# Stores of prepared weights, moved from the load queue (SyncE) to ScalarE's queue, behind the next unit's sign

## The chip, the cores and the metric

The kernel runs on one core of one Trainium2 chip. The metric is the device time of one execution in microseconds (us), given as the median of three runs. Beside it stands one profiled execution, with the times of every instruction on the engines: PE (TensorE, with PEld for its weight loads), DVE (VectorE), ACT (ScalarE), POOL (GpSimd) and SP (SyncE, whose instructions issue DMAs). A queue name with a q (SPq, ACTq) is an engine's sequencer, which issues DMAs.

## The reference

A soft-capped attention, a gated MLP on its output, and a second MLP with a cosine. All weights of the MLPs arrive as float64 pairs of words and are turned into float32 on the chip.

```python
scores = cap * np.tanh(scale * np.matmul(q, k.transpose(0, 1, 3, 2)) / cap)
attn = softmax(scores)                      # written out in the source, with + 1e-09
x = np.matmul(attn, v)                      # (4, 12, 448, 64) -> 1792 tokens x 768
gate = 1.0 / (1.0 + np.exp(-(x @ w_gate)))  # 768 x 1536
y = gate * (x @ w_val) @ w_out              # 1536 x 768
h = y @ w_in                                # 768 x 2048
out = (h * np.cos(h)) @ w_out2              # 2048 x 768
```

## The kernel before

The tokens are done in two halves of 896 (hf 0 and 1). The order of work, written out by hand, is: attention of half 0, first MLP of half 0 with attention of half 1 beside it, **first MLP of half 1 with the "background" beside it**, second MLP of half 1, second MLP of half 0. Matmuls run in pairs of high and low parts: every weight tile w has a high part (w[:, 0]) and a low part (w[:, 1]), and for each slice of 128 rows mm3 issues four matmuls with the high part and then two with the low part.

The weights are cut into 70 units of up to 128 x 768. Units 0 to 35 belong to the first MLP, units 36 to 69 (w_in as wi, w_out2 as wz) to the second. In the first pass a unit is loaded raw (768 KB, two words for each weight), converted, and the result is stored to a DRAM tile kept[u] (384 KB), from which the later half reads it back (`w_load`, tiles f) instead of converting it again. For units 36 to 69 this conversion is the work of `background()`: it runs one step at a time between the matmuls of the first MLP of half 1, in the seven places BESIDE_G of each gate and value tile and the nine places BESIDE_Y of each output tile, and what is left runs when that MLP is over. A unit takes four steps:

1. Abs of the raw words on ACT (L158) into a float tile fb.
2. Sign of the raw words in place on ACT (L160), and then the raw load of the next unit (L149, on SP).
3. Two conversions on DVE (L165, L167).
4. Two more on DVE (L171, L175).

The store of the unit before (L205) stands in step 1, behind the Abs of the next unit, on SP's queue. Its DMA waits for L175 of the unit that it stores.

At the same time the main line reads the stored units back: `w_load` (L142) brings f from kept; `w_split` makes the high part on ACT (L238) and the low part on POOL (L239), which give the weight tile w that PE uses. In the first MLP of half 1, w60 to w71 are the twelve half tiles of its output matmul (py, 36 matmuls each), and w72, w73, w74 belong to the first three hidden tiles (ph) of the second MLP. Each half of py ends with a `w_step`, which splits one more w and loads one more f.

Tiles f and fb share one pool of four buffers (FB = 4), so a new f or fb waits for the last reader of the buffer that it gets: a POOL subtraction (L239) where an f was in it, the landing of a store (L205) where an fb was. Which buffer it gets is settled when the program is built; the count that an instruction's wait names tells it. Raw tiles and w share a pool of seven. Each engine and each queue works its instructions off in the order of the program: an instruction that waits holds up all behind it.

After the output matmul of each tile m of half 1, ACT casts y (L590) and DVE subtracts (L591); ph of the second MLP needs all six y. Each ph is copied by ACT (h, L707), scaled (u, L684), rounded on DVE (L685, L686), and goes through a sine on ACT (L691, its table loaded first) before the next cast of a w.

Of the kernel before, what the change touches and what calls it, by code (L numbers as in the profile page):

```python
# [27 lines left out]
def softcap_attention_gated_mlp_cos_mlp(  # L28
# [18 lines left out]
    nc = tc.nc  # L47
# [77 lines left out]
    kept = [dram.tile([P, UW], F32, tag=f"kept{i}", name=f"kept{i}") for i in range(NU)]  # L125
# [6 lines left out]
    def f_tile(i):  # L132
        return fpool.tile([P, UW], F32, tag="f", name=f"f{i}")
# [12 lines left out]
    def raw_tile(u):  # L146
        name, src, nk, n = u
        t = wts.tile([P, UW, 2], I32, tag="w", name=f"{name}_raw")[:, : nk * n]
        nc.sync.dma_start(out=t.rearrange("p (k f) t -> p k f t", k=nk), in_=src)  # L149
        return t  # L150
# [5 lines left out]
    def signs(raw, g):  # L156
        hi = raw[..., 1].bitcast(F32)
        nc.scalar.activation(out=g, in_=hi, func=AF.Abs)  # L158
        yield
        nc.scalar.activation(out=hi, in_=hi, func=AF.Sign, bias=tiny)  # L160

    def convert(raw, g):
        lo, hi = raw[..., 0], raw[..., 1]
        gi = g.bitcast(I32)
        nc.vector.tensor_scalar(out=g, in0=g, scalar1=F64_MIN_HI, scalar2=F64_MAX_HI, op0=ALU.max, op1=ALU.min)  # L165
        yield
        nc.vector.tensor_scalar(  # L167
            out=gi, in0=gi, scalar1=4, scalar2=REBIAS, op0=ALU.logical_shift_left, op1=ALU.bitwise_xor
        )
        yield  # L170
        nc.vector.scalar_tensor_tensor(  # L171
            out=gi, in0=lo, scalar=28, in1=gi, op0=ALU.logical_shift_right, op1=ALU.bitwise_or
        )
        yield
        nc.vector.scalar_tensor_tensor(  # L175
            out=gi, in0=gi, scalar=1, in1=hi, op0=ALU.logical_shift_right, op1=ALU.bitwise_xor
        )
# [20 lines left out]
    def background():  # L198

        raw = {N1: raw_tile(unit[N1])}  # L200
        done = None

        def store():
            u, g = done
            nc.sync.dma_start(out=kept[u][:, : g.shape[1]], in_=g)  # L205
            there.add(u)

        yield
        for u in range(N1, NU):
            _, _, nk, n = unit[u]  # L210
            g = f_tile(f"b{u}")[:, : nk * n]
            c = signs(raw[u], g)
            next(c)
            if done:
                store()
            yield
            for _ in c:
                pass
            if u + 1 < NU:
                raw[u + 1] = raw_tile(unit[u + 1])  # L220
            yield
            c = convert(raw.pop(u), g)
            next(c)
            next(c)
            yield
            for _ in c:
                pass
            done = (u, g)
            yield
        store()  # L230

    def w_split():
# [493 lines left out]
    with tc.manual_schedule():  # L726
        nc.vector.memset(zeros, 0.0)
        nc.vector.reciprocal(out=tanh_scale, in_=cap_sb)
        nc.vector.tensor_scalar_mul(out=tanh_scale, in0=tanh_scale, scalar1=1.0 / float(D) ** 0.5)
        nc.scalar.activation(out=guard, in_=cap_sb, func=AF.Exp, scale=-1.0)  # L730
        nc.vector.tensor_scalar_mul(out=guard, in0=guard, scalar1=1e-9 / CP)
        att = [attention(hf) for hf in range(B // BH)]
        steps = 3 + (BH * NP + 1) * NC - LAST
        for _ in range(steps):
            next(att[0])
        mlp1(0, att[0], att[1])
        for _ in range(steps - len(BESIDE)):
            next(att[1])
        others = background()
        lead[0] = 2  # L740
        y = mlp1(1, att[1], others)
        y_first = []
        for _ in others:
            pass
        lead[0] = 3
        mlp2(1, y, y_again(y_first))
        mlp2(0, y_first, iter(()))
# [35 lines left out]
```

## Time and profile before

| | us |
|---|---|
| median of 3 runs (1223.87 to 1224.69) | 1224.36 |
| the profiled execution's own time | 1220.99 |
| its span, first to last instruction | 1219.2 |
| PE busy in the span | 1195.7 (98%) |
| DVE, ACT, POOL busy | 687.5, 592.3, 445.6 |

The profiled execution is 3.4 us under the median of the runs, and 1.8 us of it lie outside the span. TensorE's granted clock is 0.998 of full speed over the span. A busy share is a mean over stages; what a change in one stage is worth is read from the waits of that stage.

### The profile page before, as it was taken

The page shows a single profiled execution, that of the slowest core. Times are in us where ns is not written, and L with a number is a line of the kernel's source. Part 1 is how long each engine was busy: PE and PEld are TensorE (multiplying, and loading weights), DVE is VectorE, ACT ScalarE, POOL GpSimd, SP SyncE. Part 2 cuts the span into 40 slices and gives each one's busy share as a digit, 9 for nine tenths or more (in the row PEclk, how much of TensorE's full clock was granted, in tenths as well). Part 3 has the DMA queues.
Part 4 walks back from the last instruction along what each step waited for, and adds up shares of the span by engine and source line. Part 5 has one row for each costly group of instructions (what it writes and reads, how often), then busy time and mean ns, then how long its engine had stood idle before and what let it go on. Part 6 is the DMA issues. An engine that isn't in the chain of part 4 may idle for free.

```text
span 1219.2 us, 15898 instructions
## 1 busy us (share of the span) xinstructions
PE 1195.7 (98%) x6347; PEld 1033.7 (85%) x6347; DVE 687.5 (56%) x729; ACT 592.3 (49%) x664; POOL 445.6 (37%) x234
## 2 busy tenths in 40 slices
PE   8989999999999999999999998999999999999998
PEld 4444889999987555999999997899999999999998
DVE  6998688778732997556566574511514534024242
ACT  6886455444425885444444345533506345344250
POOL 2767123223314665223233222522514333335140
PEclk9999999999999999999999999999999999999999
DMA  6431565555833340275655674121211631213003
GB/s 157 124 99 49 163 219 166 168 168 169 231 131 104 86 135 4 90 225 177 220 169 188 212 231 160 55 65 43 64 59 33 200 104 46 72 33 100 18 27 98
DMA packets 127083, 148.17 MB, mean 122 GB/s; under 512 B 50081, under 2 KB 100641, under 8 KB 127009
## 3 DMA queue, kind: packets, MB, share of 16 engines
q1 hardware_dynamic: 126720, 147.09, 39.1%
q8 instruction: 50, 0.82, 0.3%
q14 instruction: 25, 0.20, 0.0%
q10 hardware_dynamic: 288, 0.07, 0.0%
HBM read 112.13 MB, written 35.00 MB: 121 GB/s over the span
## 4 chain that ended last, share of the span: by engine, by line
PE 75%; DVE 13%; ACT 4%; DMA 4%; issue 2%; SPq 1%; POOL 0%; DVEq 0%; ACTq 0%; POOLq 0%
PE po L638 17%; PE ph L517 16%; PE pg L517 13%; PE pv L517 12%; PE py L517 7%; PE pv L422 4%; PE s L393 3%; DVE r L441 2%; DMA wz_raw<-in_moe_w_out_dram 2%; PE more L638 1%; PE t L372 1%; DVE f L171 1%; PE den L438 1%; DMA wi_raw<-in_moe_w_in_dram 1%; DVE fb L171 1%
## 5 line engine op out<-in xcount | busy, mean ns | idle before, releaser
L239 POOL TENSOR_TENSOR w<-f,w 128x768 fp32r<-128x768 f32 (+1 forms) x140 | 269.5, 1931 | 662.4 <-ACT w L238 572.8
L638 PE MATMUL po<-w,z 128*128 128x384 f32 x1248 | 221.0, 335 | 1.9 <-POOL w L239 1.9
L638 PEld LDWEIGHTS po<-w,z 128*128 128x128 f32 x1248 | 216.8, 188 | 2.9 <-POOL w L239 2.8
L517 PE MATMUL pv<-x,w 128*128 128x448 f32 x864 | 180.0, 366 | 0.9 <-DVE sg L566 0.9
L517 PE MATMUL pg<-x,w 128*128 128x448 f32 x864 | 179.9, 366 | 0.0
L517 PE MATMUL py<-g,w 128*128 128x448 f32 x864 | 177.5, 366 | 0.0
L517 PEld LDWEIGHTS pv<-x,w 128*128 128x128 f32 x864 | 162.0, 188 | 15.9 <-issue 3.0
L517 PEld LDWEIGHTS pg<-x,w 128*128 128x128 f32 x864 | 162.0, 188 | 14.7 <-ACT p L396 0.7
L517 PEld LDWEIGHTS py<-g,w 128*128 128x128 f32 x864 | 161.7, 188 | 13.5 <-issue 1.0
L685 DVE TENSOR_SCALAR n<-u 128x896 f32<-128x896 f32 (+1 forms) x38 | 29.4, 773 | 181.6 <-ACT u L684 181.6
L238 ACT CAST w<-f 128x768 fp32r<-128x768 f32 (+1 forms) x140 | 112.2, 809 | 39.3 <-DVE f L175 16.2
L517 PE MATMUL ph<-y,w 128*128 128x448 f32 (+1 forms) x578 | 119.9, 369 | 3.3 <-ACT y L590 2.8
L517 PEld LDWEIGHTS ph<-y,w 128*128 128x128 f32 x578 | 109.3, 190 | 13.3 <-ACT y L590 3.2
L517 PE MATMUL ph<-ya,w 128*128 128x448 f32 (+2 forms) x579 | 118.2, 365 | 0.0
L517 PEld LDWEIGHTS ph<-ya,w 128*128 128x128 f32 x579 | 108.4, 188 | 9.1
L396 ACT ACTIVATE p<-s,tanh_scale 112x896 f32<-112x896 f32 x96 | 93.0, 1011 | 43.0 <-PE s L393 42.9
L402 ACT ACTIVATE p<-p,cap_sb 112x1792 f32<-112x1792 f32 x48 | 86.3, 1798 | 0.1
L393 PEld LDWEIGHTS s<-st 64*112 64x112 f32 x576 | 45.7, 171 | 40.9 <-ACT p L396 19.0
L422 PE MATMUL pv<-p,v 112*64 112x448 f32 x384 | 77.5, 545 | 2.7 <-PE t L372 2.7
L441 DVE RECIPROCAL r<-den 128x448 f32<-128x448 f32 x24 | 70.8, 2950 | 8.7 <-PE den L438 8.7
L393 PE MATMUL s<-st 64*112 64x448 f32 x576 | 73.3, 380 | 1.5 <-ACT p L396 1.4
L406 POOL TENSOR_TENSOR sum<-p 112x896 f32<-112x896 f32 x24 | 55.9, 2330 | 49.1 <-ACT p L402 24.1
(82 smaller groups left out, 1201.8 us busy)
## 6 DMA issues: line engine op xcount, KB each, us to landing
f<-kept SPq DMA_DIRECT2D x96, 384.0 KB, 3.1
kept<-f SPq DMA_DIRECT2D x36, 384.0 KB, 2.7
wi_raw<-in_moe_w_in_dram SPq DMA_DIRECT2D x16, 768.0 KB, 5.8
kept<-fb SPq DMA_DIRECT2D x30, 384.0 KB, 2.7
wz_raw<-in_moe_w_out_dram SPq DMA_DIRECT2D x14, 768.0 KB, 5.2
wg_raw<-in_moe_w_gate_dram SPq DMA_DIRECT2D x12, 768.0 KB, 4.9
wv_raw<-in_moe_w_val_dram SPq DMA_DIRECT2D x12, 768.0 KB, 5.2
wo_raw<-in_moe_w_out_dram SPq DMA_DIRECT2D x12, 768.0 KB, 4.8
```

The lines of the kernel that those rows point to most:

```text
L171: nc.vector.scalar_tensor_tensor(out=gi, in0=lo, scalar=28, in1=gi, op0=ALU.logical_shift_right, op1=ALU.bitwise_or)
L238: nc.scalar.copy(out=t[:, 0], in_=r)
L239: nc.gpsimd.tensor_tensor(out=t[:, 1], in0=r, in1=t[:, 0].bitcast(F32), op=ALU.subtract)
L393: nc.tensor.matmul(ps[:CP, h, :S], lhsT=st[r, ki, ks], rhs=st[r, qi], start=(n == 0), stop=(n == 2))
L396: nc.scalar.activation(out=pt[:CP, j], in_=ps[:CP, :, :S], func=AF.Tanh, scale=tanh_scale[:CP])
L402: nc.scalar.activation(out=pt[:CP], in_=pt[:CP], func=AF.Exp, scale=cap_sb[:CP])
L406: nc.gpsimd.tensor_tensor(out=s, in0=pt[:CP, 1] if half == 0 else s, in1=pt[:CP, 0], op=ALU.add)
L422: nc.tensor.matmul(pv[h * D : (h + 1) * D, :S], lhsT=tv[:, h, c, :], rhs=pt[:CP, j, h, :], start=(c == 0), stop=(c == NC - 1),)
L441: nc.vector.reciprocal(out=r[:, 0], in_=den[:, :S])
L517: nc.tensor.matmul(ps[:, c, s0:s1], lhsT=w[:, wi, kk, :], rhs=x[:, xi, c, s0:s1], start=(first and (wi, xi) == (0, 0)), stop=(last and (wi ...
L638: nc.tensor.matmul(pos_t[t][:, :NB], lhsT=zf[kk][:, zi, t * P : (t + 1) * P], rhs=ws[kk // UK][:, wi, kk % UK, :], start=(kk == 0 and (zi, ...
L685: nc.vector.tensor_scalar_add(out=n[:, c], in0=u[:, c], scalar1=ROUND)
```

## The change

The store's DMA is issued by ScalarE (`nc.scalar`) and no longer by SyncE, and it moves in the program from behind the Abs of the next unit to behind its Sign, one step later. Nothing is added or taken away: the same 34 stores move the same bytes.

```diff
         def store():
             u, g = done
-            nc.sync.dma_start(out=kept[u][:, : g.shape[1]], in_=g)
+            nc.scalar.dma_start(out=kept[u][:, : g.shape[1]], in_=g)
             there.add(u)
...
             c = signs(raw[u], g)
             next(c)
+            yield
+            for _ in c:
+                pass
             if done:
                 store()
-            yield
-            for _ in c:
-                pass
             if u + 1 < NU:
                 raw[u + 1] = raw_tile(unit[u + 1])
             yield
```

What the built programs show at three places. Names: f and w carry their place in the sequence, fb and kept the number of the unit, wz_1_1_2_raw is a raw tile; behind "waits" stand the semaphores, DMAHW for the landing of a DMA, Pool, DVE, PE and Activation for an engine's progress.

**Place 1: ACT, at the end of the first gated tiles of half 1 (unit 55 follows w61).** Before:

```order
L238 CAST w61_5276<-f61_5172 128x768 [waits DMAHW4_49]
L158 ACTIVATE fb55_5288<-wz_1_0_4_raw_5248 128x384 [waits DMAHW2_49,DMAHW0_49]
L160 ACTIVATE wz_1_0_4_raw_5248<-wz_1_0_4_raw_5248,tiny_165 128x384 [waits Activation_49]
L238 CAST w62_5328<-f62_5223 128x768 [waits DMAHW6_49]
L158 ACTIVATE fb56_5339<-wz_1_1_0_raw_5304 128x768 [waits DMAHW3_49,Pool_49]
```

Now:

```order
L238 CAST w61_5276<-f61_5171 128x768 [waits DMAHW4_49]
L158 ACTIVATE fb55_5288<-wz_1_0_4_raw_5248 128x384 [waits DMAHW7_49,DMAHW6_49,Pool_49]
L160 ACTIVATE wz_1_0_4_raw_5248<-wz_1_0_4_raw_5248,tiny_165 128x384 [waits Activation_49]
L205 DMA kept54_135<-fb54_5232 128x768 [waits DMAHW3_49]
L238 CAST w62_5328<-f62_5223 128x768 [waits DMAHW6_49]
L158 ACTIVATE fb56_5339<-wz_1_1_0_raw_5304 128x768 [waits DMAHW3_49,DMAHW2_49]
```

The store of unit 54 now stands between the Sign of unit 55 and the cast of w62. Since that store is issued later, the buffer of fb54 is not there for fb55: its Abs waited for the landing of kept54 and for its raw load, and waits now for POOL, by its count for the subtraction of w61.

**Place 2: SP, the loads around the raw load of unit 57 (wz_1_1_2).** Before:

```order
L142 DMA f64_5331<-kept28_109 128x768 [waits DMAHW4_49,Pool_49]
L205 DMA kept55_136<-fb55_5288 128x384 [waits DMAHW5_49,DVE_49]
L149 DMA wz_1_1_2_raw_5349<-in_moe2_w_out_dram 128x2x768 [waits DMAHW6_49]
L205 DMA kept56_137<-fb56_5339 128x768 [waits DMAHW7_49,DVE_49]
L142 DMA f65_5385<-kept29_110 128x768 [waits DMAHW1_49,DMAHW0_49,Pool_49]
```

Now:

```order
L149 DMA wz_1_1_0_raw_5304<-in_moe2_w_out_dram 128x2x768 [waits DMAHW2_49,Activation_49]
L142 DMA f64_5331<-kept28_109 128x768 [waits DMAHW6_49,DMAHW4_49,Pool_49]
L149 DMA wz_1_1_2_raw_5349<-in_moe2_w_out_dram 128x2x768 [waits DMAHW5_49,DVE_49]
L142 DMA f65_5384<-kept29_110 128x768 [waits DMAHW7_49,DMAHW1_49,Pool_49]
L149 DMA wz_1_1_4_raw_5398<-in_moe2_w_out_dram 128x768 [waits DVE_49]
```

The raw load stands directly behind the load of f64 and no longer behind the store of unit 55. By the counts of its waits f64 waited for the subtraction of w61 and waits now for that of w62, one tile later. For f65 and f66 the subtraction that they wait for is the same in both programs (w63, w64). In the same way f72 waits now for the subtraction of w70 (before: the landing of kept63) and f73 for that of w71 (before: the landing of kept65).

**Place 3: ACT, the end of the background, before the first hidden tile of the second MLP.** Before:

```order
L160 ACTIVATE wz_2_1_2_raw_5883<-wz_2_1_2_raw_5883,tiny_165 128x768 [waits Activation_49]
L238 CAST w73_5925<-f73_5819 128x768 [waits DMAHW2_49]
L590 CAST y1_5_5930<-py1_5_5824 128x896 [waits PE_49]
L158 ACTIVATE fb69_5937<-wz_2_1_4_raw_5923 128x384 [waits DMAHW1_49,DMAHW0_49,Pool_49]
L160 ACTIVATE wz_2_1_4_raw_5923<-wz_2_1_4_raw_5923,tiny_165 128x384 [waits Activation_49]
L707 COPY h1_0_5983<-ph1_0_5946 128x896 [waits PE_49]
```

Now:

```order
L160 ACTIVATE wz_2_1_2_raw_5883<-wz_2_1_2_raw_5883,tiny_165 128x768 [waits Activation_49]
L205 DMA kept67_148<-fb67_5862 128x768 [waits DVE_49]
L238 CAST w73_5925<-f73_5818 128x768 [waits DMAHW1_49]
L590 CAST y1_5_5930<-py1_5_5823 128x896 [waits PE_49]
L158 ACTIVATE fb69_5937<-wz_2_1_4_raw_5923 128x384 [waits DMAHW7_49,DMAHW0_49]
L160 ACTIVATE wz_2_1_4_raw_5923<-wz_2_1_4_raw_5923,tiny_165 128x384 [waits Activation_49,Pool_49]
L205 DMA kept68_149<-fb68_5913 128x768 [waits DVE_49]
L205 DMA kept69_150<-fb69_5937 128x384 [waits DVE_49]
L707 COPY h1_0_5983<-ph1_0_5946 128x896 [waits PE_49]
```

One store stands now ahead of the casts of w73 and y1_5, and two ahead of the copy of h1_0; the last of them waits for DVE's conversion of unit 69, which no instruction of ACT waited for before.

## Rows read from the trace of the kernel before

**Rows 1.** The page: part 1 (busy us), and the stores in part 6.

```profile
PE 1195.7 (98%) x6347; PEld 1033.7 (85%) x6347; DVE 687.5 (56%) x729; ACT 592.3 (49%) x664; POOL 445.6 (37%) x234
...
kept<-fb SPq DMA_DIRECT2D x30, 384.0 KB, 2.7
```

**Rows 2.** Timeline of PE: start, length, instructions merged, idle before and releaser.

```profile
651.27 87.71 PE L517 MATMUL py<-g,w 128*128 128x448 f32 x432
738.82 6.24 PE L517 MATMUL ph<-y,w 128*128 128x448 f32 x30
747.88 0.67 PE L517 MATMUL ph<-y,w 128*128 128x448 f32 x2 [2.82 <-ACT y L590]
...
758.78 29.90 PE L517 MATMUL ph<-y,w 128*128 128x448 f32 x144
```

**Rows 3.** Windows: busy us of PE, PEld, DVE, ACT, POOL; granted clock, DMA.

```profile
750.00:753.00 3.00, 3.00 (x10) 2.66 (x9) 2.86 (x6) 2.66 (x4) 0.00 (x0) 0.52 0.06 24
```

**Rows 4.** Waits of SP's queue: total us, times, longest.

```profile
SPq L205 <- DVE fb L175: 118.4, 30, 13.0
```

**Rows 5.** Timeline of SP's queue: start, length of the issue.

```profile
661.12 0.32 SPq L205 DMA_DIRECT2D kept<-fb  x1
661.49 0.43 SPq L149 DMA_DIRECT2D wz_raw<-in_moe_w_out_dram  x1
...
718.92 0.32 SPq L142 DMA_DIRECT2D f<-kept  x1
721.81 0.32 SPq L205 DMA_DIRECT2D kept<-fb  x1
722.22 0.38 SPq L149 DMA_DIRECT2D wz_raw<-in_moe_w_out_dram  x1
...
728.38 0.32 SPq L142 DMA_DIRECT2D f<-kept  x1
...
738.25 0.44 SPq L149 DMA_DIRECT2D wz_raw<-in_moe_w_out_dram  x1
```

**Rows 6.** Timeline of ACT at units 55 and 59 and behind the last y.

```profile
655.58 0.56 ACT L158 ACTIVATE fb<-wz_raw 128x384 f32<-128x384 f32 x1
...
685.57 0.82 ACT L238 CAST w<-f 128x768 fp32r<-128x768 f32 x1
...
746.93 0.90 ACT L590 CAST y<-py 128x896 fp32r<-128x896 f32 x1
...
750.54 0.91 ACT L707 COPY h<-ph 128x896 f32<-128x896 f32 x1 [0.33 <-PE ph L517]
751.34 1.01 ACT L684 ACTIVATE u<-ph,quarter 128x896 f32<-128x896 f32 x1
...
756.47 0.82 ACT L238 CAST w<-f 128x768 fp32r<-128x768 f32 x1
```

**Rows 7.** Timeline of POOL: subtractions of w61 and w62, w65, w70, w71, w74.

```profile
655.72 3.90 POOL L239 TENSOR_TENSOR w<-f,w 128x768 fp32r<-128x768 f32 x2 [7.93 <-ACT w L238]
...
686.47 1.85 POOL L239 TENSOR_TENSOR w<-f,w 128x768 fp32r<-128x768 f32 x1 [9.12 <-ACT w L238]
...
718.99 1.98 POOL L239 TENSOR_TENSOR w<-f,w 128x768 fp32r<-128x768 f32 x1 [4.42 <-ACT w L238]
727.35 1.86 POOL L239 TENSOR_TENSOR w<-f,w 128x768 fp32r<-128x768 f32 x1 [6.39 <-ACT w L238]
...
757.37 2.03 POOL L239 TENSOR_TENSOR w<-f,w 128x768 fp32r<-128x768 f32 x1 [8.45 <-ACT w L238]
```

**Rows 8.** Timeline of DVE: the end of the background and the first rounding.

```profile
753.36 0.56 DVE L175 SCALAR_TENSOR_TENSOR fb<-fb,wz_raw 128x384 int32<-128x384 int32 x1
753.83 0.62 DVE L685 TENSOR_SCALAR n<-u 128x896 f32<-128x896 f32 x1
```

**Rows 9.** Timeline of ACT's queue at the start: the only two DMAs that it issues.

```profile
0.74 0.39 ACTq L323 DMA_DIRECT2D ident<-in_eye_dram  x1
1.17 0.52 ACTq L327 DMA_DIRECT2D cap_sb<-in_cap_dram  x1
```

More of the change, by code (lines that the diff above doesn't have):

```diff
@@ L213, in background @@
             next(c)
-            if done:
-                store()
             yield
@@ L218, in background @@
                 pass
+            if done:
+                store()
             if u + 1 < NU:
```

## The prediction

> **What bounds the kernel now.** The page comes first: PE is busy 98% of the span [rows 1], so a change gains only where PE waits, and loses where it makes PE wait. The change touches the stretch from 497 us, the first background store, to 754 us, the last. In PE's timeline there is then one wait to be seen: the output matmul (py) runs through from 651.27 us, the first hidden tile (ph) begins at 738.82, and after 30 matmuls PE stands for 2.82 us until ACT has cast the last y [rows 2]. Behind that wait the granted clock is 0.52 in the window of 750 to 753, the lower of TensorE's two levels (1.2 of 2.4 GHz); ten matmuls run there instead of the 14.8 that 3 us hold at the pace below, some 1.0 us lost [rows 3]. More is not to be won here than these 3.8 us.
>
> What can be lost is read from margins. 432 matmuls of py start over 738.82 - 651.27 = 87.55 us, 0.2027 us each, so every half tile of 36 takes 7.30 us and w65, the sixth, is wanted at 651.27 + 5 x 7.30 = 687.75, its low part four matmuls later at 688.56 [rows 2]. The low part of w65 is ready at 686.47 + 1.85 = 688.32 [rows 7]: 0.24 us to spare. Likewise w74: wanted at 758.78, low part at 759.59 [rows 2], ready at 757.37 + 2.03 = 759.40 [rows 7]: 0.19 us. So the weights come just in time, and the question is whether ACT and POOL make them later.
>
> They follow a chain that goes round once for each half tile: a POOL subtraction ends and frees a buffer; SP loads an f into it and, 0.37 us behind, the next raw unit; the raw lands; ACT does Abs; only then, in its order, comes the next cast of a w, and POOL's next subtraction. The last turn shows it: a raw load is issued at 738.25 [rows 5], and the cast of the last y, which stands on ACT behind that unit's Abs, comes at 746.93 [rows 6], while PE waits.
>
> **The change part by part.**
>
> The issue. 34 stores leave SP's queue, 0.32 us each [rows 5], and with them SP's 118.4 us of waiting for DVE ahead of them [rows 4]. ACT gets 34 issues of 0.39 to 0.52 us, as its two at the start took [rows 9]; I take 0.4. 34 x 0.4 = 13.6 us in all, hidden in ACT's idle half, save where a store stands between Abs and a cast that PE waits for. The transfers themselves, 2.7 us to landing [rows 1], stay.
>
> What a store waits for on ACT. It waits for L175 of the unit before, which is mostly done when the Sign of the next is; nothing is added there, except at the end of the background (third step below).
>
> First step, the chain up to w65. The store is issued one step later, so its buffer comes free later, and the program gives f and fb other buffers. The Abs of unit 55 ran at 655.58 [rows 6]; it now waits for w61's subtraction, which ends at 655.72 + 1.95 = 657.67 (half of two, [rows 7]): 2.09 us later. With kept54's issue (0.4) behind it, w62's subtraction ends at 659.62 + 2.5 = 662.1, and f64 waits for that now. The raw load behind f64 goes at 662.1 + 0.05 + 0.37 = 662.5, where it went at 661.49, behind the store of 661.12 [rows 5]: 1.0 us late. For f65 and f66 nothing changes, so the delay goes through to w65, plus 0.4 for kept58's issue ahead of its cast: 1.4 us, the lower bound. Upstream of w61 the same exchange of buffers takes place; the largest one that I can read is f72's, 718.92 to the end of w70's subtraction at 720.97 [rows 5, 7], 2.05 us, so 3.5 us is the upper bound. I take the middle, 2.4. Then w65's high part is ready at 685.57 + 0.82 + 2.4 = 688.79 [rows 6], PE waits 1.0 us, and its low part at 690.72 while PE would want it at 689.60: 1.1 more. PE is 2.2 us late.
>
> Second step, the last y. f73 waits now for w71's subtraction, 727.35 + 1.86 = 729.21 [rows 7], where it went at 728.38 [rows 5]: 0.83 us, and the raw load, w72 and the next turn follow it. kept67's issue stands ahead of y's cast: 0.4. Nothing else late: 1.2 us, the lower bound. At f72 something is given back: its raw load went at 722.22, behind the store of 721.81 [rows 5]; now it goes at 720.97 + 0.4 = 721.4, 0.8 us sooner, plus whatever w70 is late. With 3.5 us late there: 3.5 - 0.8 + 0.83 + 0.4 = 3.9 us, the upper bound. I take the middle, 2.5 us. What PE lost at w65 doesn't add to this: PE comes to the place of the 2.82 us wait later by 2.2, y is later by 2.5, and it waits 3.1 there. The low clock behind it stays.
>
> Third step, w74. kept69 now waits on ACT for the conversion of unit 69, which ends at 753.36 + 0.56 = 753.92 [rows 8], and the copy of h1_0, which ran at 750.54 [rows 6], stands behind it: 753.92 + 0.05 + 0.4 = 754.37, 3.8 us later. u follows 0.80 later and takes 1.01 [rows 6], so the rounding starts at 756.18 and not at 753.83, when DVE came free of the background [rows 8]: 2.35 us later. From there to w74's cast it is as before, so its high part is ready at 756.47 + 0.82 + 2.35 = 759.64 [rows 6] and not by 758.78: PE waits 0.86. The low part is ready at 761.75, and wanted at 759.64 + 0.81 = 760.45: 1.3 more. Together 2.1 us, on top of the second step, because all these times move with y.
>
> The sum: 2.5 + 2.1 = 4.6 us. On the profiled execution, 1220.99, that is 1225.6; on the median of the runs, which lies 3.4 us above it, 1224.36 + 4.6 = 1229.0 us, 0.38% slower.
>
> On the transfers the Trainium skill (DMA: Bandwidth & Descriptors, section Issuing engines are not separate DMA queues) says that DMAs issued by ScalarE and SyncE end up on the same 16 DMA engines, and that a second issuer saves only the sequencer's time. No row before shows a store from ACT. By that sentence alone nothing would move in or out of PE's path, and the time would stay at 1224.4.
>
> **The rivals.**
>
> No change (0.26). Between the raw loads of units 57 and 68 there are twelve on the chain. If each lands 0.25 us sooner because no store sits right ahead of it on its queue, as at 721.81 and 722.22 [rows 5], the chain gets 3 us back: y is 0.5 us early, the third step still costs 2.1, and the time is 1226.0. For it: SP's waits for DVE are gone [rows 4]. Against it: f loads stand in the same place ahead of the raw loads, and on the rows read they now wait for a later subtraction.
>
> Faster (0.14), the same mechanism with more effect. By the first two sums total = delay of y + 2.1 us, since w74 hangs on the same chain. For a gain over 2.45 us, the 0.2% that a measurement here can tell from no change, y must be 4.6 us sooner than before, 7.1 us better than forecast, or 0.6 us for each of the twelve loads. Then 1221.8; the most is 1220.6, with all of the 3.8 us won. The skill (same page, section Queues, rings and completion order) says that SP and ACT each have a ring of their own on every DMA engine, served in turn packet by packet, by which a store would share with a raw load and not delay it as a whole; no run here shows it.
>
> Slower still (0.12). The first step at its upper bounds, y 3.9 us late, and a further stretch of low clock behind the new waits at w65 and w74, 1.0 us each as in [rows 3]: 3.9 + 2.1 + 2.0 = 8.0, 1232.4 us.
>
> **How the numbers follow.** The forecast itself, 2.5 to 7 us slower, has 0.48; with the rival beyond it slower has 0.60, the same 0.26, faster 0.14. The lower bounds of the terms (1.2 + 2.1) give 1227.7, the upper ones (3.9 + 2.1) 1230.4. The range for 8 in 10 takes in most of "no change" and the low clock: 1223.0 to 1233.5.
>
> **What the changed profile would show.** Step one right: PE waits of 1 us or more for the cast and the subtraction of w65 near 688 us; wrong: py without a gap. Step two right: the wait for the last y stays near 3 us and ends at 750 instead of 747.9; wrong: it is shorter, or the y cast comes before 746.9. Step three right: the copy of h1_0 stands behind the last two stores, and PE waits for w74; wrong: no wait for w there. The prediction fails as a whole if raw loads of the y stretch land in clearly less time than now, or if the store's issue on ACT takes far from 0.4 us.

## The result, and the profile after the change

The change makes the kernel slower. Five executions of the changed kernel have a median of 1233.78 us (1230.11 to 1236.21), five of the kernel before on the same chip 1224.69 us (1223.87 to 1226.86): 9.1 us by the medians. The ratio, estimated from all the executions and so not the quotient of the two medians (1.0074), is 1.0063 (95% interval 1.0048 to 1.0078), or 7.7 us. In all comparisons, executions that took over 1.5% longer than the fastest of the same kernel are left out. The forecast was 1229.0 us, 4.6 us slower, with a range up to 1233.5. The sign was right, and so were the places that it named. The size was 50 to 60% of what came; the median lies 0.3 us above the range, and the time by the ratio (1232.1) inside it. The profiled execution after took 1233.04 us (span 1231.2), 12.0 us more than the span before.

The page, parts 1 and 6: PE has 7.7 us more busy time, some of it matmuls at the low clock, and the stores are now issued by ACT's queue. They land a little sooner than before (2.3 us, where [rows 1] have 2.7).

```profile
PE 1203.4 (98%) x6347; PEld 1036.4 (84%) x6347; DVE 690.1 (56%) x729; ACT 592.3 (48%) x664; POOL 446.6 (36%) x234
...
kept<-fb ACTq DMA_DIRECT2D x30, 384.0 KB, 2.3
```

The timeline of PE after the change, the answer to [rows 2] (start, length, matmuls merged, idle before and releaser):

```profile
530.13 6.75 PE L517 MATMUL pv<-x,w 128*128 128x448 f32 x32 [0.46 <-POOL w L239]
545.21 6.75 PE L517 MATMUL pv<-x,w 128*128 128x448 f32 x32 [0.21 <-POOL w L239]
604.83 6.75 PE L517 MATMUL pv<-x,w 128*128 128x448 f32 x32 [0.86 <-POOL w L239]
...
655.19 37.04 PE L517 MATMUL py<-g,w 128*128 128x448 f32 x180
694.13 1.09 PE L517 MATMUL py<-g,w 128*128 128x448 f32 x4 [1.90 <-ACT w L238]
696.04 52.09 PE L517 MATMUL py<-g,w 128*128 128x448 f32 x248 [0.82 <-POOL w L239]
747.97 6.24 PE L517 MATMUL ph<-y,w 128*128 128x448 f32 x30
757.40 0.83 PE L517 MATMUL ph<-y,w 128*128 128x448 f32 x2 [3.19 <-ACT y L590]
...
769.21 1.08 PE L517 MATMUL ph<-y,w 128*128 128x448 f32 x4 [1.10 <-ACT w L238]
771.31 28.99 PE L517 MATMUL ph<-y,w 128*128 128x448 f32 x134 [1.02 <-POOL w L239]
```

Before, there was one wait in this stretch, beside the 0.45 us for DVE's part of the same y (0.30 now, in neither count). Now there are eight: three in the value tiles of the gated MLP, two at w65 (its high part 2.5 us late: 694.13 against 655.19 + 180 x 0.2027 = 691.68; its low part 1.1 more), the old one for the last y, and two at w74. Behind three of them TensorE runs at the lower of its two levels (1.2 of 2.4 GHz). Windows of the changed kernel, columns as in [rows 3]:

```profile
696.50:699.50 3.00, 3.00 (x10) 2.69 (x9) 2.92 (x4) 0.23 (x1) 0.00 (x0) 0.50 0.77 215
758.00:761.00 3.00, 2.70 (x8) 2.21 (x8) 2.90 (x5) 0.55 (x1) 0.45 (x1) 0.50 0.40 130
771.50:774.50 3.00, 3.00 (x9) 2.65 (x10) 1.45 (x2) 1.48 (x2) 3.00 (x2) 0.50 0.45 134
```

Where the 12.0 us of the profile arise is read from the same places in the two timelines:

| place | before | after | late by |
|---|---|---|---|
| gate tile ahead of the first background store | 490.76 | 491.49 | 0.73 |
| py starts | 651.27 | 655.19 | 3.92 |
| ph starts | 738.82 | 747.97 | 9.15 |
| PE gets the last y | 747.88 | 757.40 | 9.52 |
| PE gets w74's low part (before 758.78 + 4 x 0.2027) | 759.59 | 771.31 | 11.72 |

The first 0.73 us lie ahead of anything that the change touches, and some 0.7 us more are matmuls that ran at a slower pace until 529 us (below). So about 2.5 us are lost in the gated tiles, 5.2 in py, 0.4 at the last y and 2.2 at w74.

### The profile page after: what moved, and what is told of

Same layout as the page of the kernel before. It is cut to its first block, busy times and chain, and to the rows that moved or that the text cites. A ratio compares the mean times of both kernels' runs of the same rounds, so it can differ in the third digit from the quotient of the medians.

```text
span 1231.2 us, 15898 instructions
## 1 busy us (share of the span) xinstructions
PE 1203.4 (98%) x6347; PEld 1036.4 (84%) x6347; DVE 690.1 (56%) x729; ACT 592.3 (48%) x664; POOL 446.6 (36%) x234
## 4 chain that ended last, share of the span: by engine, by line
PE 66%; DVE 10%; DMA 8%; issue 6%; ACT 5%; POOL 3%; SPq 1%; ACTq 0%; POOLq 0%; DVEq 0%
PE po L638 17%; PE ph L517 16%; PE pv L517 8%; PE pg L517 8%; PE py L517 7%; DMA wz_raw<-in_moe_w_out_dram 4%; PE pv L422 4%; PE s L393 3%; POOL w L239 2%; DMA kept<-fb 2%; DMA wi_raw<-in_moe_w_in_dram 1%; DVE r L441 1%; PE more L638 1%; PE t L372 1%; ACT p L396 1%
```

## Where the chain falls behind first

The prediction began its first step at unit 55. The first slip stands 140 us earlier. Two loads on SP's queue, first in the kernel before and then in the changed one, with POOL's two subtractions of the changed kernel (w42 and w43):

```profile
515.91 0.32 SPq L142 DMA_DIRECT2D f<-kept  x1
...
522.81 0.32 SPq L142 DMA_DIRECT2D f<-kept  x1
```

```profile
518.31 0.34 SPq L142 DMA_DIRECT2D f<-kept  x1
...
530.11 0.32 SPq L142 DMA_DIRECT2D f<-kept  x1
```

```profile
515.73 2.55 POOL L239 TENSOR_TENSOR w<-f,w 128x768 fp32r<-128x768 f32 x1 [4.20 <-ACT w L238]
528.12 1.96 POOL L239 TENSOR_TENSOR w<-f,w 128x768 fp32r<-128x768 f32 x1 [9.84 <-ACT w L238]
```

The two f are f44 and f45. Before, by the counts of their waits, they got the buffers of fb37 and fb38 once those stores had landed, with the subtractions of w40 and w41 long done. When the program allots f44 now, the store of unit 37 has not been written yet, so f44 gets the buffer of f42 and waits for w42's subtraction: 515.73 + 2.55 = 518.28, and it goes at 518.31, 2.4 us late. The raw load stands behind it, the Abs behind the raw load, the cast of w43 behind the Abs: it comes at 527.15 and not at 523.52, and its subtraction ends at 530.08. PE is waiting for it (530.13 in the timeline above), and so is f45: 7.3 us late, and its raw load with it. Of these 7.3 us, 3.65 are the exchange at the old times (w43's subtraction ended at 526.46 before, and f45 went at 522.81); the other 3.6 are w43's own lateness. In that, 2.4 us come from the raw load that went later (518.70 and not 516.28), and 1.2 from its landing: its Abs starts 6.8 us behind the issue, 5.6 before. So transfers have a smaller part in it beside the buffers. By the wait counts the same exchange comes back eight units later at f52 and f53, at f60 and f61, at f64, and in the output matmul's stretch at f67, f69, f71, f72 and f75, each of which now waits for the subtraction of the w two before it (f73 too, see place 2).

## The experiments

Each ratio is against the kernel before on the same chip, five rounds. The spread of these is wider than in the first comparison; where an interval decides nothing, the waits of the trace are read.

| | place of the store | queue | other | ratio | 95% interval |
|---|---|---|---|---|---|
| change | behind Sign | ACT | | 1.0063 | 1.0048 to 1.0078 |
| 1 | old | ACT | | 1.0003 | 0.9980 to 1.0026 |
| 2 | behind Sign | SP | | 1.0097 | 1.0064 to 1.0130 |
| 3 | behind Sign | ACT | five f/fb buffers | 0.9941 | 0.9916 to 0.9966 |
| 4 | old | SP | five f/fb buffers | 0.9945 | 0.9919 to 0.9970 |
| 5 | behind Sign | ACT | last store on SP | 1.0018 | 0.9999 to 1.0037 |
| 5, again | | | | 1.0038 | 1.0021 to 1.0054 |
| 6 | old | ACT | last store on SP | 0.9979 | 0.9957 to 1.0001 |
| 7 | one step sooner than old | ACT | | 1.0016 | 0.9999 to 1.0032 |
| 8 | one step later than behind Sign | ACT | | 1.0045 | 1.0024 to 1.0066 |
| 9 | behind Sign up to unit 54, then old | ACT | | 1.0025 | 1.0006 to 1.0043 |
| 10 | old up to unit 54, then behind Sign | ACT | | 1.0022 | 1.0011 to 1.0032 |
| 11 | old | ACT | last two stores on SP | 0.9997 | 0.9979 to 1.0015 |

**1. The queue alone** (the only difference to the kernel before):

```diff
-            nc.sync.dma_start(out=kept[u][:, : g.shape[1]], in_=g)
+            nc.scalar.dma_start(out=kept[u][:, : g.shape[1]], in_=g)
```

> Half of the change: the store is issued on ScalarE, at its old place behind the Abs of the next unit. Theory P (place: the store comes a step later, its buffer comes free later, f and fb get other buffers, and the chain of raw loads is late by some microseconds): the chain is as before, only the last stores still stand ahead of the copy of h1_0, so 2.1 us: 1226.8, with the last y near 747 us and a PE wait for w74. Theory Q (queue: a store that waits for DVE on ACT holds up the casts behind it): a store that stands one step sooner waits for DVE longer, so at least as slow as the whole change, 1234 or more.

No change: 1.0003. The timeline of PE:

```profile
744.45 15.27 PE L517 MATMUL ph<-y,w 128*128 128x448 f32 x72
762.01 1.08 PE L517 MATMUL ph<-y,w 128*128 128x448 f32 x4 [2.29 <-ACT w L238]
764.11 30.47 PE L517 MATMUL ph<-y,w 128*128 128x448 f32 x140 [1.02 <-POOL w L239]
```

There is no wait for w in the gated tiles or in py, and none for the last y, which even [rows 2] have; the two waits at w74 are there. Two things weaken this reading. The execution ran at the slower of two paces that are told of at the end (py in 89.44 us, 87.71 in [rows 2]), so PE came later to the last y; run 6, the same program up to its last store, ran py in 87.71 us and waited 0.96 us for it. And the queue is not quite alone: in the built program 22 of the 174 f and fb tiles lie in another buffer than before (41 with the change), f47 to f49 and f55 to f57 among them. What is won here is won by the queue together with an allotment of its own. Theory Q falls: of stores that wait for DVE on ACT, the ratio and PE's waits show nothing but the third step. Theory P had the place right, but not that the chain would gain what the third step costs.

**2. The place alone** (the store on SyncE, but behind the Sign):

```diff
             c = signs(raw[u], g)
             next(c)
-            if done:
-                store()
             yield
             for _ in c:
                 pass
+            if done:
+                store()
```

> The other half: the store stays on SyncE, but stands behind the Sign, one step later. Theory P: the last y is late as in the whole change, the third step (the stores ahead of h1_0 on ACT) is gone: 1224.7 + 9.1 - 2.1 = about 1231. Theory Q: nothing waits on ACT for DVE, so 1224.7.

The slowest of all: 1.0097, some 12 us (its interval, 1.0064 to 1.0130, overlaps the change's). Theory Q falls; theory P has the direction right, and the size is above it. PE has six waits in the value tiles, of which the longest is shown, three in py (0.51, 1.72 and 0.82 us), and then the one for the last y:

```profile
610.40 6.75 PE L517 MATMUL pv<-x,w 128*128 128x448 f32 x32 [1.01 <-POOL w L239]
...
765.16 11.28 PE L517 MATMUL ph<-y,w 128*128 128x448 f32 x46 [4.12 <-ACT y L590]
```

So the late place costs, and by the ratios ACT's queue gives a part of it back. The exchange of buffers alone does not explain this run: in its program f44, f45, f52, f53, f60 and f61 change their buffers as with the change, but f64, f67, f69, f71, f72 and f75 have those of the kernel before. What is late there has to come from ahead, or from stores that land later. Also, store and raw load go out directly behind each other on one queue; the stores land in 4.0 us (2.7 before, 2.3 with the change) and the raw loads of the wz units in 6.0 (5.2 and 5.1). That this slower landing has a part in the 12 us is a rival that no run rules out.

**3 and 4. A fifth buffer for f and fb**, with the change and without it:

```diff
-    FB = 4
+    FB = 5
...
-    small = ctx.enter_context(tc.tile_pool(name="small", bufs=6))
+    small = ctx.enter_context(tc.tile_pool(name="small", bufs=4))
```

> The whole change with five f and fb buffers and not four (the small pool of the attention goes from 6 to 4 tiles to make room; the run of the kernel before with the same two pools is its control). Theory P: with a fifth buffer f and fb no longer wait for a store that comes late; only the third step is left, so 2.1 us over the control. Theory Q: the stores stand where they stood on ACT, so 9 us over the control.

> Control: the kernel before with five f and fb buffers and a small pool of 4. Both theories: the chain of the kernel before is just in time, so a fifth buffer wins back at most the 2.8 us wait for the last y and the 1.0 us of low clock behind it: 1221 to 1225; the smaller pool of the attention may cost something ahead of 465 us, which the start of the gated tiles of half 1 (471 us) shows.

Both are faster than the kernel before, 0.9941 and 0.9945, and the difference of 8 to 9 us between change and no change is gone, within intervals of 3 us either way. With the fifth buffer the late store keeps no one waiting: the timeline of PE with the change has py and 216 matmuls of ph without a gap, and ACT copies h1_0 when PE has made it, since the last conversion is done by then. A fifth buffer would hide a slower landing as well; that the buffers are the path is read at f44 and f45 above.

```profile
658.34 89.44 PE L517 MATMUL py<-g,w 128*128 128x448 f32 x432
747.62 44.80 PE L517 MATMUL ph<-y,w 128*128 128x448 f32 x216
```

```profile
752.93 2.25 ACTq L205 DMA_DIRECT2D kept<-fb  x2
755.26 0.91 ACT L707 COPY h<-ph 128x896 f32<-128x896 f32 x1 [5.39 <-PE ph L517]
```

Not even the third step is left, which theory P had wanted at 2.1 us. The timeline of run 4:

```profile
655.07 87.71 PE L517 MATMUL py<-g,w 128*128 128x448 f32 x432
742.62 43.94 PE L517 MATMUL ph<-y,w 128*128 128x448 f32 x216
786.39 1.40 PE L638 MATMUL po<-w,z 128*128 128x384 f32 x7
```

and the end of the same stretch in the kernel before, which begins at 738.82 [rows 2]:

```profile
788.52 1.38 PE L638 MATMUL po<-w,z 128*128 128x384 f32 x7
```

The 216 matmuls of ph take 43.77 us in run 4 and 49.70 before. So the wait for the last y, with what follows it (DVE's part of y, the low clock), cost the kernel before 5.9 us, and not the 3.8 that the prediction and the expectation of run 4 took for the most to be won. By its ratio run 4 gains some 6.7 us.

These are the only two versions clearly faster than the kernel before. The smaller pool of the attention was not run by itself; in run 4's profile py starts 3.8 us later than before.

**5. The change with the last store back on SyncE**, run twice; the trace read is that of the second time.

```diff
-        def store():
+        def store(q=nc.scalar):
             u, g = done
-            nc.scalar.dma_start(out=kept[u][:, : g.shape[1]], in_=g)
+            q.dma_start(out=kept[u][:, : g.shape[1]], in_=g)
...
-        store()
+        store(nc.sync)
```

> The whole change, but the last store alone (unit 69) goes back to SyncE, so that no instruction of ACT ahead of the copy of h1_0 waits for DVE's last conversion. Theory P (chain late by the buffers, plus the third step): the wait for the last y stays at about 3 us, the two waits for w74 (1.1 and 1.0 us in the changed kernel) and the low clock behind them (1.7 us) go: 3 to 4 us under the changed kernel, ratio to the kernel before 1.003. Rival R (w74 is late because its own f or its own subtraction is late, not because of the copy): the waits for w74 stay, and the time is that of the change, ratio 1.006.

> The change with the last store alone back on SyncE, once more, for an undisturbed trace (the first one held a run of 6110 us). Theory P: the copy of h1_0 comes some 3 us sooner after the last y than in the changed kernel, w74 is waited for by under 1 us or not at all, the wait for the last y stays near 3 us; ratio 1.002 to 1.003, as measured the first time. Rival R: waits for w74 as in the changed kernel (1.1 and 1.0 us).

1.0018 and 1.0038, under the change's 1.0063 both times, though the second interval (1.0021 to 1.0054) reaches into the change's. ACT in the changed kernel, from the Sign of unit 68 on:

```profile
754.86 0.97 ACT L160 ACTIVATE wz_raw<-wz_raw,tiny 128x768 f32<-128x768 f32 x1
754.87 0.33 ACTq L205 DMA_DIRECT2D kept<-fb  x1
755.74 0.81 ACT L238 CAST w<-f 128x768 fp32r<-128x768 f32 x1
756.46 0.90 ACT L590 CAST y<-py 128x896 fp32r<-128x896 f32 x1
...
761.56 2.25 ACTq L205 DMA_DIRECT2D kept<-fb  x2
763.85 0.91 ACT L707 COPY h<-ph 128x896 f32<-128x896 f32 x1 [5.30 <-DVE fb L175]
...
768.34 0.82 ACT L238 CAST w<-f 128x768 fp32r<-128x768 f32 x1
```

and in run 5, second time:

```profile
754.50 0.90 ACT L590 CAST y<-py 128x896 fp32r<-128x896 f32 x1
...
759.97 0.91 ACT L707 COPY h<-ph 128x896 f32<-128x896 f32 x1 [3.35 <-DVE fb L165]
...
764.47 0.82 ACT L238 CAST w<-f 128x768 fp32r<-128x768 f32 x1
```

From the last y to the cast of w74 it is 11.88 us with the change, 9.97 with the last store moved back, and 9.54 before [rows 6]. PE's waits at w74 are gone, those at w65 (2.2 and 0.8 us) and for the last y (3.2 us) are not. Rival R falls, and the third step is shown by itself.

**6 and 11. The queue alone, with the last store, or the last two, back on SyncE**: the same edit of `store` and of its last call as in 5, on run 1; for 11 the call in the loop is also `store(nc.sync if u == NU - 1 else nc.scalar)`.

> Queue alone (store on ScalarE at its old place), but the last store goes back to SyncE. With the queue alone the last y was not waited for, and w74 was, for 2.29 and 1.02 us. Theory P: both waits are gone, 3.3 us and the low clock behind them, some 4 to 5 us under the queue alone: ratio 0.996 to 0.997, faster than both kernels. Rival R: w74 is late by its own chain, the waits stay, ratio 1.000.

> Stores on ScalarE at the old place, the last two (units 68 and 69) on SyncE. With one alone moved back, the last y was waited for by 0.96 us and w74 still by 0.91 and 1.02 us, since kept68 stood ahead of the copy of h1_0. Theory P: with both gone w74 comes about 1 us sooner; PE's waits fall from 2.9 to about 1 us, 1 to 2 us under that run: ratio 0.996 to 0.997. Rival R: w74 is late by its own f or by DVE, which the stores on ACT don't touch: ratio 0.998.

0.9979 and 0.9997, neither clearly different from the kernel before, and neither as fast as theory P wanted. PE in run 6, and then in run 11:

```profile
746.61 0.67 PE L517 MATMUL ph<-y,w 128*128 128x448 f32 x2 [0.96 <-ACT y L590]
...
757.01 1.07 PE L517 MATMUL ph<-y,w 128*128 128x448 f32 x4 [0.91 <-ACT w L238]
759.10 28.64 PE L517 MATMUL ph<-y,w 128*128 128x448 f32 x140 [1.02 <-POOL w L239]
```

```profile
747.73 0.66 PE L517 MATMUL ph<-y,w 128*128 128x448 f32 x2 [2.07 <-ACT y L590]
```

In run 6 the wait for the last y falls from 2.82 us to 0.96, so the queue does win 1.9 us on the chain (0.8 in the execution of run 11). SP's queue shows from where: the raw load of [rows 5] that went at 722.22, behind a store, goes here at 719.42, right behind its f.

```profile
719.04 0.34 SPq L142 DMA_DIRECT2D f<-kept  x1
719.42 0.42 SPq L149 DMA_DIRECT2D wz_raw<-in_moe_w_out_dram  x1
```

But PE then comes to w74 sooner, and w74 is no sooner, so the waits there take the place of the one removed. In run 11 w74's cast came as theory P wanted (9.57 us behind y), but the time did not fall: the last y was waited for by 2.07 us in that execution, and w74's low part still by 1.00. Neither theory comes out as written, and the times of the two runs can't be told apart.

**7 and 8. One step sooner, one step later.** In 7 the call of `store` stands behind `done = (u, g)`, and in 8 behind the first two conversions of the next unit, both on ACT.

> Queue alone, and the store one step sooner than before (right behind its unit's last conversion, ahead of the next unit's Abs on ACT). Theory P: buffers come free no later than before, so no wait for the last y; the last store still stands ahead of h1_0, w74 is waited for as with the queue alone: ratio 1.000. Theory Q (a store that waits for DVE on ACT holds up what stands behind it): all 34 now stand right behind the conversion that they wait for and ahead of the Abs that frees the next raw load, so the Abs is late by the conversion's length, some 2 to 4 us for each unit; the chain then falls behind and the ratio is 1.01 or more.

> The whole change with the store one step later still (behind the first two conversions of the next unit). Theory P: each step later keeps a buffer for one step more; the step from the old place to the new cost 0.6% (ratio 1.0003 with the queue alone, 1.0063 with the change), a further one costs as much or more: 1.012 or over, with waits of py for w and a longer wait for the last y. Rival S (the new place happened to get a bad order of buffers, and lateness itself is nothing): no trend, 1.000 to 1.006.

1.0016 and 1.0045. Run 7 is as run 1, within the intervals, and theory Q falls once more, although the stores held ACT up for longer at the end: w74's high part was waited for by 3.45 us, 2.29 in run 1. Run 8 is not slower than the change: that lateness costs the more, the longer it is, is wrong. Its PE waits are at the places of the change, with one in the value tiles (0.47 us) in place of three, and the one for y smaller:

```profile
696.55 1.08 PE L517 MATMUL py<-g,w 128*128 128x448 f32 x4 [2.35 <-ACT w L238]
...
759.22 0.67 PE L517 MATMUL ph<-y,w 128*128 128x448 f32 x2 [1.53 <-ACT y L590]
```

By the wait counts, f67 to f73 and f75 get their buffers behind the same subtractions in both programs. So the loss seems to go with the reader that a load has to wait for, and not with the store's own delay; that is argued from the counts, since no run sets the buffers by hand, and run 2, the slowest although most of these loads have their old readers there, shows that it can't be the whole. Theory P in its plain form falls, and rival S has a part of the truth.

**9 and 10. The new place for the early units, or for the late ones.**

```diff
+            if done and not (u <= 54):
+                store()
             yield
             for _ in c:
                 pass
-            if done:
+            if done and u <= 54:
                 store()
```

(run 9; in run 10 the condition is `u > 54`)

> Stores all on ScalarE; in the iterations up to unit 54 (the gated tiles, and ahead of w61) at the new place, from unit 55 on at the old one. Theory L (the prediction's: the chain loses at f64 and f73, in the output matmul's stretch, and what is late ahead of it is caught up): no wait for the last y, as with the queue alone, ratio 1.000 to 1.001. Theory U (upstream: f45 and f47, which go 7 and 10 us later in the changed kernel than before, make w late in the gated tiles, and PE loses some 2 to 3 us there that nothing gives back): waits of pv for POOL's w, ratio 1.002 to 1.004.

> The complement: old place up to unit 54, new place from unit 55 on. Theory L: the whole loss of the new place is here, the last y is late as in the whole change: ratio 1.006. Theory U: no waits in the gated tiles, the rest of the loss: ratio 1.003 to 1.004.

1.0025 and 1.0022: each half costs about 3 us, with intervals of 1 to 2 us either way, and neither alone costs what the whole does. PE in run 9, where the lateness brought from upstream meets w65 and the last y although the stores there stand at the old place, and then in run 10:

```profile
692.34 1.09 PE L519 MATMUL py<-g,w 128*128 128x448 f32 x4 [1.71 <-ACT w L240]
...
753.91 0.68 PE L519 MATMUL ph<-y,w 128*128 128x448 f32 x2 [1.50 <-ACT y L592]
```

```profile
751.50 0.67 PE L519 MATMUL ph<-y,w 128*128 128x448 f32 x2 [1.78 <-ACT y L592]
```

In run 10 py has no gap at all, and only the last y and w74 are waited for. A part of that is the slower pace (py in 88.46 us). But run 10 and the change both begin py at 655.19, and the cast of w65 ends at 691.10 in run 10 and at 694.08 with the change. So 3 us of the lateness at w65 come from units ahead of 55; at the pace of [rows 2] PE would have waited in run 10 for w65's low part, ready at 693.04, by some 0.5 us (an estimate from these rows). Theory L, all of it in the late stretch, falls. Theory U has the first half right; the second is a little less than it said.

## Why the prediction was right and wrong

**What held.** The chain of raw loads does go late through the buffers, and for the larger part not through the transfers, and PE waits where it was said: for w65, for the last y, for w74. The last y: the wait was to stay near 3 us (3.1) and end later; it is 3.19. That the number fits is in part luck: PE came to that place 9.15 us late and not 2.2, and y 9.5 us and not 2.5, two terms that were both some 7 us too small and cancel in the wait. **The third step** was forecast from [rows 6] and [rows 8] at 2.35 us from the last y to w74's cast and at 2.1 us of PE time. The cast came 11.88 - 9.54 = 2.34 us later, and PE lost 11.72 - 9.52 = 2.2; run 5 takes the step away alone.

**What was mis-sized: the second step, the last y 2.5 us late between bounds of 1.2 and 3.9.** In the profile the last y is 9.52 us late; without the 0.73 us ahead of the change and the 0.7 us of slower matmuls it is about 8, by the medians 9.1 - 2.2 = 6.9, and by the ratio 7.7 - 2.2 = 5.5: over the upper bound by each of them. What failed is that bound: upstream of w61 "the same exchange of buffers takes place; the largest one that I can read is f72's", 2.05 us. That was read from one place behind unit 55 and carried to all places ahead of it. f45 is 7.3 us late, more than three times that figure. A subtraction is no fixed delay: it stands itself behind a cast, behind an Abs and behind a raw load that was put off by the load before, so two exchanges in a row (f44 late by 2.4 us, then f45 by 7.3) add up to more than either row shows. Runs 9 and 10 divide the loss: the units ahead of 55 cost about as much as those behind, and there the prediction priced nothing in PE time and did not foresee the waits in the value tiles, some 2.5 us in the profile.

**The first step** (w65) was put at 2.2 us of PE time; it took 2.45 + 1.1, and 1.7 more at the low clock behind it (248 matmuls in 51.93 us, where 50.27 are due). That stretch, and the one behind w74, were part of the rival "slower still" (1232.4 us). It was given 0.12 and came nearest to the result. The low clock was priced at 1.0 us from one window of 3 us [rows 3], which is too little: 1.7 here, and behind the last y of the kernel before, by run 4, some 2.

**The issue on ACT** was priced at 0.4 us in front of a cast. It takes 0.33, and in the rows above it runs beside the Sign (754.86 and 754.87): from that Sign's start to the next cast it is 0.88 us, as in the kernel before (745.33 to 746.21). In these rows an issue that finds its data ready costs nothing; one that has to wait holds ACT up, as at 761.56.

**The rival "no change"** was right in its mechanism and wrong in its place in the sum. Raw loads did not land sooner (5.1 us for the wz units after, 5.2 before; 6.3 and 5.8 for the wi units), but where only the queue changes they are issued sooner, and the chain wins 1.9 us in run 6's profile, 0.8 in run 11's. Runs 1 and 2 fit this: by the ratios the late place costs 12 us on SP's queue, and on ACT's some 7 (1.0063 against 1.0003). The Trainium skill (DMA: Bandwidth & Descriptors, section Issuing engines are not separate DMA queues) says that a second issuer saves the sequencer's time alone. The runs agree as far as the kernel before goes: raw loads land no sooner, and what was won is time of SP's queue, most of it waiting. Against run 2, with the stores at the same place on SP, the raw loads of the wz units do land 0.9 us sooner with the change, and those of the wi units 0.3 later (6.0 and 6.3). By that sentence alone the whole change would have cost nothing; it is silent on the buffers, and the loads at f44 and f45, and runs 3 and 4, show that they matter more here.

**What stays open:** how the loss of the place is shared between loads that wait for a later subtraction and Abs instructions that wait for a later landing. Both come from the same allotment, and no run separates them, nor the part that slower landings have. The queue, too, changes the allotment, so runs 1 and 2 don't divide the loss cleanly between queue and place.

## What to carry to other kernels

When an instruction that ends a buffer's use is moved later, ask first who is allotted that buffer, and then which instruction the next owner waits for instead; with a pool as tight as this one (four buffers for two kinds of tile) that outweighs what the move itself costs or saves. Bound such an exchange at its first place in the program and not at the one that is easiest to read, since each late load puts off the one that frees the next. And where one more buffer can be found, it can be worth more than either order: with one taken from another stage's pool both versions are 0.5 to 0.6% faster than the kernel before.

## What the runs showed of the hardware

The same matmuls run at two paces at a granted clock of 1.00. In runs 3 and 4, shown above, py's 432 matmuls run without a wait in 89.44 us and in 87.71, 2% apart; the window of each:

```profile
658.00:747.00 89.00, 89.00 (x432) 80.84 (x431) 55.95 (x59) 38.75 (x47) 25.87 (x13) 1.00 0.66 220
```

```profile
655.00:742.00 87.00, 87.00 (x431) 80.62 (x430) 54.82 (x59) 36.58 (x45) 23.70 (x12) 1.00 0.64 211
```

The pace changes within a run too. In the changed kernel the half tiles from 491 to 529 us start 7.44 us apart, and later ones 7.30; one row of each:

```profile
491.49 7.60 PE L517 MATMUL pg<-x,w 128*128 128x448 f32 x36
...
559.09 7.46 PE L517 MATMUL pv<-x,w 128*128 128x448 f32 x36
```

What sets it no run here shows. It is why the spans of single profiles are not compared here without the waits: run 3 has no waits in this stretch and yet a span of 1222.6 us, 4.9 more than run 4.

A second thing came and went without the change. A stretch at the low clock near 51 us stands in the changed kernel (granted clock 0.89 from 45 to 60 us, 1.00 before), and in runs 1, 3, 4, 6, 8, 9, 10 and 11 as well (0.91 from 40 to 60 us), and not in runs 2 and 7 or in run 5's second trace; the first background store comes some 440 us later. Whether it is a part of the 0.73 us by which the profile after was late ahead of the change is open: run 2, without it, came to the same place at 493.79 us, 2.3 us later still.
